# A scan-and-experts kernel: the first block laid out anew

The first of six blocks of a fused kernel gets another order of loads, gates, scans and weight sums, and some buffers of its own.

## The chip, the cores and the metric

One core of one Trainium2 chip. The metric is the device time of one execution in microseconds (us), the median of several runs. The profiled execution has a span some 1.7 us below its run's time.

## The reference, cut to what matters

```python
# batch 4, 8 heads, 768 positions, head_dim 32, state 16
for each chunk: y = (C B^T * decay_mask) x + C state * decay; state = decay_full * state + B^T x * decay
x = y rearranged to (3072, 256)
p = probs / (probs.sum(-1) + 1e-9)
out = sum over 4 experts e of p[:, e] * (relu(x @ w1[e]) @ w2[e])      # w1: 256x1024, w2: 1024x256
```

All in fp32.

## The kernel before

Tokens are handled in 24 chunks of 128 positions; four chunks are a block. The first block's chunks 0 to 3 are computed first. Then come 48 steps; each does half an expert for one block with seven products in place of eight for each of the two multiplications (sums and differences of the quarters are multiplied). Step n does the seven products of its own first multiplication (`fmul`, into the accumulator banks X and Y) and seven of the second multiplication of step n−1 (`smul`). During steps 0 to 7 the chunks of the next block are computed in between: a chunk "enters" in one step (decays, scores, masking) and "leaves" in a later one (outputs, state). The weights' sums are made by GpSimd in the first block, two steps ahead, and stored for the later blocks.

The names: `LT` is the decay mask of a chunk, made by a scan on VectorE; `bdec` and `cts` are two products of it on GpSimd; `masked` multiplies the scores into it; `sums` makes `yS`, the differences of the block's input quarters; `snap` is a copy by ScalarE (ACT).

```python
    def load_decays(c, queue):
        ab = load.tile([P, NH * P], FP32, tag="ab", name="ab")
        ah = load.tile([HN, P], FP32, tag="ah", name="ah")
        cut, whole = (a, a) if c < DIRECT else (acut_d, ac_d)
        nc.sync.dma_start(out=ab, in_=cut[c].rearrange("h s -> (h s)").partition_broadcast(P))
        queue.dma_start(out=ah, in_=whole[c].unsqueeze(1).to_broadcast([NH, N, P]))
        st[c].update(ab=ab, ah=ah)
    # ...
    def sum_weights(n):

        if n >= SPB:
            return
        for op in (lambda w: wt1[n][:, w].rearrange("p (j m) -> p j m", j=JJ),
                   lambda w: w2_op(n, w)):
            nc.gpsimd.tensor_add(op(S1), op(S3), op(A22))
            nc.gpsimd.tensor_sub(op(S2), op(S1), op(A11))
            nc.gpsimd.tensor_sub(op(S4), op(A12), op(S2))
            nc.gpsimd.tensor_sub(op(S3), op(A11), op(S3))
        nc.gpsimd.dma_start(out=w1_d[n], in_=wt1[n])
        nc.gpsimd.dma_start(out=w2_d[n], in_=wt2[n])
    # ...
    def decays(c):
        s = st[c]
        if c < DIRECT:
            clip(s["ab"])
            nc.vector.memset(s["ab"].rearrange("p (h s) -> p h s", h=NH)[:, :, 0:1], 0.0)

        LT = att.tile([P, NH * P], FP32, tag="LT", name="LT")
        nc.vector.tensor_tensor_scan(
            out=LT, data0=s["ab"], data1=ident.rearrange("p h s -> p (h s)"), initial=0.0,
            op0=ALU.mult, op1=ALU.add)
        s["LT"] = LT.rearrange("p (h s) -> p h s", h=NH)

        if c < DIRECT:
            clip(s["ah"])

        s["dec"] = dec = att.tile([HN, P], FP32, tag="dec", name="dec")
        nc.vector.tensor_tensor_scan(
            out=dec, data0=s["ah"], data1=zeros, initial=1.0, op0=ALU.mult, op1=ALU.add)
        s["bdec"] = bdec = att.tile([P, NH, N], FP32, tag="bdec", name="bdec")
        nc.gpsimd.tensor_mul(
            bdec, s["xb"][:, OB:OB + HN].rearrange("p (h n) -> p h n", h=NH),
            s["LT"][:, :, P - 1:P].to_broadcast([P, NH, N]))
        s["cts"] = cts = att.tile([HN, NT, P], FP32, tag="cts", name="cts")
        nc.gpsimd.tensor_mul(cts, s["ctm"], dec.unsqueeze(1).to_broadcast([HN, NT, P]))
    # ...
    def masked(c, qs):
        s = st[c]
        for q in qs:
            h = slice(NT * q, NT * q + NT)
            nc.vector.tensor_mul(s["LT"][:, h], s["g"][q], s["LT"][:, h])
    # ...
    def fmul(n, i):

        k = n // SPB
        f = first.setdefault(n, {})
        bank = "X" if i in (1, 6, 7, 4) else "Y"
        if i in (1, 2, 5):
            f[bank] = ps_f.tile([P, JJ, HB], FP32, tag=bank, name=bank)
        y, Y = yT[k], yS[k]
        w = (A11, A12, S4, A22, S1, S2, S3)[i - 1]
        b1, b2 = slice(0, HB), slice(HB, BLK)
        rhs = (y[:, 0, b1], y[:, 1, b1], y[:, 1, b2], Y[:, 3], Y[:, 0], Y[:, 1], Y[:, 2])[i - 1]
        for j in range(JJ):
            nc.tensor.matmul(
                out=f[bank][:, j], lhsT=wt1[n][:, w, j * P:j * P + P], rhs=rhs,
                start=(i in (1, 2, 5) and j == 0), stop=(j == JJ - 1), skip_group_check=True)
    # ...
    def total(n, i, b):

        z = first[n]["z" + b] = ffn.tile([P, JJ, HB], FP32, tag="z", name="z", bufs=3)
        nc.vector.tensor_add(z, first[n]["Y"], first[n][i])

    def gated(n, b, src):

        if n not in hid:
            hid[n] = {}
        h = hid[n][b] = ffn.tile([P, JJ, HB], FP32, tag="h" + b, name="h" + b)
        k, e = n // SPB, n % SPB // JJ
        half = int(b[1]) - 1
        g = gate[k, e].rearrange("p c s -> p (c s)")[:, half * HB:half * HB + HB]
        nc.vector.scalar_tensor_tensor(
            out=h, in0=first[n][src], scalar=0.0, in1=g.unsqueeze(1).to_broadcast([P, JJ, HB]),
            op0=ALU.max, op1=ALU.mult)

    def diff(n, o, x, y):
        h = hid[n]
        h[o] = ffn.tile([P, JJ, HB], FP32, tag="h" + o, name="h" + o)
        nc.vector.tensor_sub(h[o], h[x], h[y])
    # ...
    for c in range(CPB):
        masks(c)
        scores(c, [(ps_s, f"acc{q}") for q in range(NQ)])
        decays(c)
        added(c, ps_f, "X")
        masked(c, range(NQ))
        outputs(c, ps_f, "Y")
        carry(c)
        if c == 0:
            load_decays(1, nc.sync)
            sum_weights(0)
        if c == 1:
            gates()
            sum_weights(1)
        if c == 2:
            load_gate(0, 0)
        load_chunk(c + 2)
    sums(0)

    both = nc.sync, nc.sync
    for n in range(NS + 1):
        k, r = divmod(n, SPB)
        i, odd = divmod(r, 2)
        c = CPB * (k + 1) + i
        more = c < NCH
        ending = r == 0 and k > 0
        run = n < NS
        if run:
            e = r // JJ
            if r % JJ == 0 and n + JJ < NS:
                load_gate(*divmod(n // JJ + 1, E))
            if n + 2 < NS:
                load_weights(n + 2)
                sum_weights(n + 2)
            fmul(n, 1)
            snap(n, 1)
            fmul(n, 2)
            total(n, 1, "11")
            gated(n, "11", "z11")
        if more and not odd:
            masks(c)
            decays(c)
        if r == 1 and k > 0:
            leave(k - 1, 0, BLK, both)
        smul(n - 1, 1)
        if run:
            fmul(n, 6)
            snap(n, 6)
        smul(n - 1, 3)
        if ending:
            keep(k - 1, 0)
        if more and odd:
            outputs(c, ps_att, "att")
            added(c, ps_att, "att")
        if run:
            fmul(n, 5)
            fmul(n, 7)
            snap(n, 7)
            total(n, 7, "22")
        smul(n - 1, 7)
        smul(n - 1, 5)
        if ending:
            keep(k - 1, 1)
        if run:
            gated(n, "22", "z22")
        if more and odd:
            carry(c)
            if c + 2 < NCH:
                load_chunk(c + 2)
        if run:
            fmul(n, 3)
            total(n, 6, "12")
            fmul(n, 4)
            gated(n, "21", "X")
            gated(n, "12", "z12")
            if more and r == SPB - 1:
                sums(k + 1)
        smul(n - 1, 6)
        # ... (the end of a block's output: cut)
        if run:
            diff(n, "T3", "22", "12")
        smul(n - 1, 2)
        if more and not odd:
            scores(c, ((ps_att, "att"), (ps_att, "att"), (ps_f, "X"), (ps_f, "Y")))
            masked(c, (2, 3, 0, 1))
        smul(n - 1, 4)
        if run:
            diff(n, "T1", "12", "11")
            diff(n, "T2", "22", "T1")
            diff(n, "T4", "21", "T2")
        # ... (output: cut)
```

## Time and profile before

| | before |
|---|---|
| median of runs | 689.91 us |
| profiled span | 687.0 us |
| start of step 0, 1, 2, 3 | 38.02, 54.79, 70.01, 83.39 us |
| first sum of yT (`yS`) | 38.56 us |
| PE busy, VectorE busy | 644.4, 500.4 us |

The median is over four runs; the prediction had three of them, with a median of 690.4. A step's start is the start of its first product, X<-yT. The slices, stretches and waits are shown in the prediction. One more view belongs here, because the prediction did not read it: the groups of VectorE instructions in steps 1 to 3 (54.79 to 96.69 us), shapes kept apart. Columns: line, engine, operation, output<-inputs, shapes, count, busy us, mean ns of one, idle before them and releasers.

```profile
L370 DVE SCALAR_TENSOR_TENSOR h<-z,gate 128x512 f32<-128x512 f32 x9 | 8.3, 919 | 0.2
L360 DVE TENSOR_TENSOR z<-Y,snap 128x512 f32<-128x512 f32 x9 | 6.2, 686 | 8.8 <-ACT snap L355 8.4 <-PE Y L348 0.4
L377 DVE TENSOR_TENSOR hT<-h,hT 128x512 f32<-128x512 f32 x6 | 5.0, 828 | 0.2
L377 DVE TENSOR_TENSOR hT<-h,h 128x512 f32<-128x512 f32 x7 | 4.7, 699 | 0.1
```

All four move the same number of elements. The z row reads one operand from the accumulators and takes 686 ns. The rows that read two tiles of SBUF take up to 919. In this kernel that costs little, because VectorE has 8.8 us of idle time before z in the same steps.

### The profile page before, as it was taken

The numbers are of one execution on the slowest core, as the hardware profiler recorded it, in microseconds if no ns is written. First come the engines' busy times: TensorE is split into PE (matmuls) and PEld (weight loads), VectorE is DVE, ScalarE is ACT, GpSimd is POOL, SyncE is SP. The second block draws the span as 40 slices with busy tenths as digits, with TensorE's granted clock in tenths as the row PEclk, the third lists the DMA queues.
The fourth block names the chain that finished last, engine by engine and source line by source line (L and its number), as shares of the span: only waits on it lengthen the run. The fifth ranks groups of instructions, "written<-read, shape, count | busy, mean of one in ns | idle before, by whom it ended". The sixth has DMA issues, their size and how long they took to land.

```text
span 687.0 us, 9082 instructions
## 1 busy us (share of the span) xinstructions
PE 644.4 (94%) x3465; PEld 539.0 (78%) x3465; DVE 500.4 (73%) x823; ACT 116.1 (17%) x230; POOL 112.4 (16%) x161
## 2 busy tenths in 40 slices
PE   2478999999999999999999999999999999999995
PEld 1246887887888887888887888888888888888884
DVE  4875976878877768768668868769777785856654
ACT  1111111112111112211212211212111122111110
POOL 5636658202000002000002000000100000200000
PEclk9998999999999999999999999999999999999998
DMA  8778487763665464655554574753673453563301
GB/s 286 270 244 318 146 299 253 265 234 115 207 230 196 139 209 171 214 183 187 203 176 161 156 280 137 250 180 124 178 267 138 153 195 111 152 230 108 107 1 31
DMA packets 71482, 128.90 MB, mean 188 GB/s; under 512 B 29072, under 2 KB 53008, under 8 KB 71440
## 3 DMA queue, kind: packets, MB, share of 16 engines
q1 hardware_dynamic: 66232, 112.93, 49.0%
q0 software_dynamic: 2304, 14.68, 5.4%
q10 hardware_dynamic: 2904, 0.72, 0.4%
q8 instruction: 27, 0.44, 0.3%
q14 instruction: 15, 0.12, 0.1%
HBM read 110.25 MB, written 18.07 MB: 187 GB/s over the span
## 4 chain that ended last, share of the span: by engine, by line
PE 88%; DVE 3%; DMA 2%; POOL 1%; issue 0%; SPq 0%; DVEq 0%; POOLq 0%
PE acc L392 41%; PE X L348 24%; PE Y L348 18%; DMA wt<-in_w_dram 2%; PE g L256 2%; PE y L295 2%; DVE h L370 1%; PE y L288 1%; DVE LT L224 1%; DVE LT L266 0%; DVE u L412 0%; POOL wt L145 0%; POOL wt L144 0%; PE A L277 0%; POOL wt L146 0%
## 5 line engine op out<-in xcount | busy, mean ns | idle before, releaser
L360 DVE TENSOR_TENSOR z<-Y,snap 128x512 f32<-128x512 f32 x144 | 99.1, 688 | 132.2 <-ACT snap L355 110.2
L392 PE MATMUL acc<-hT,wt 128*128 128x256 f32 x768 | 191.1, 382 | 0.0
L355 ACT COPY snap<-X 128x512 f32<-128x512 f32 x144 | 84.3, 585 | 487.9 <-PE X L348 485.9
L392 PEld LDWEIGHTS acc<-hT,wt 128*128 128x128 f32 x768 | 144.3, 190 | 25.2 <-issue 6.3
L392 PE MATMUL acc<-h,wt 128*128 128x256 f32 x576 | 148.3, 380 | 4.9 <-DVE u L412 4.9
L348 PE MATMUL X<-yS,wt 128*128 128x256 f32 x576 | 147.8, 379 | 0.0
L392 PEld LDWEIGHTS acc<-h,wt 128*128 128x128 f32 x576 | 109.1, 190 | 21.9 <-DVE u L412 7.3
L348 PEld LDWEIGHTS X<-yS,wt 128*128 128x128 f32 x576 | 109.5, 190 | 14.9
L370 DVE SCALAR_TENSOR_TENSOR h<-z,gate 128x512 f32<-128x512 f32 x144 | 102.6, 712 | 3.3
L348 PE MATMUL Y<-yT,wt 128*128 128x256 f32 x384 | 100.2, 384 | 2.0 <-DVE z L360 2.0
L348 PEld LDWEIGHTS Y<-yT,wt 128*128 128x128 f32 x384 | 72.7, 193 | 14.4 <-DVE z L360 2.8
L236 POOL TENSOR_TENSOR bdec<-xb,LT 128x128 f32<-128x128 f32 x24 | 10.4, 434 | 399.8 <-issue 185.7
L377 DVE TENSOR_TENSOR hT<-h,hT 128x512 f32<-128x512 f32 x96 | 68.9, 718 | 3.3
L377 DVE TENSOR_TENSOR hT<-h,h 128x512 f32<-128x512 f32 x96 | 65.0, 701 | 1.3
L224 DVE TENSOR_TENSOR_SCAN LT<-ab,ident 128x1024 f32<-128x1024 f32 x24 | 55.7, 2323 | 3.8 <-DMA ab<-acut_d 3.7
L348 PE MATMUL X<-yT,wt 128*128 128x256 f32 x192 | 51.5, 392 | 6.7 <-DVE LT L266 6.7
L348 PE MATMUL Y<-yS,wt 128*128 128x256 f32 x192 | 51.5, 390 | 0.0
L266 DVE TENSOR_TENSOR LT<-g,LT 128x256 f32<-128x256 f32 x96 | 34.0, 416 | 20.9 <-PE g L256 12.3
L348 PEld LDWEIGHTS X<-yT,wt 128*128 128x128 f32 x192 | 37.2, 196 | 12.9 <-DVE LT L266 7.5
L348 PEld LDWEIGHTS Y<-yS,wt 128*128 128x128 f32 x192 | 34.7, 189 | 6.5 <-issue 0.8
L370 DVE SCALAR_TENSOR_TENSOR h<-X,gate 128x512 f32<-128x512 f32 x48 | 33.0, 688 | 5.6 <-PE X L348 5.5
L256 PE MATMUL g<-ctm,xb 32*128 32x256 f32 x192 | 19.9, 473 | 11.6 <-ACT ctm L247 11.5
(65 smaller groups left out, 272.8 us busy)
## 6 DMA issues: line engine op xcount, KB each, us to landing
wt<-w_d SPq DMA_DIRECT2D x80, 896.0 KB, 4.6
w_d<-wt POOLq DMA_DIRECT2D x16, 896.0 KB, 7.8
...
```

Source lines behind the costliest of these rows:

```text
L224: nc.vector.tensor_tensor_scan(out=LT, data0=s["ab"], data1=ident.rearrange("p h s -> p (h s)"), initial=0.0, op0=ALU.mult, op1=ALU.add)
L236: nc.gpsimd.tensor_mul(bdec, s["xb"][:, OB:OB + HN].rearrange("p (h n) -> p h n", h=NH), s["LT"][:, :, P - 1:P].to_broadcast([P, NH, N]))
L256: nc.tensor.matmul(out=g.rearrange("p t s -> p (t s)"), lhsT=s["xb"][k, OBT:OBT + P], rhs=s["ctm"][k].rearrange("p t s -> p (t s)"), start ...
L266: nc.vector.tensor_mul(s["LT"][:, h], s["g"][q], s["LT"][:, h])
L288: nc.tensor.matmul(out=y.rearrange("p t s -> p (t s)"), lhsT=state["M"].rearrange("p q d -> p (q d)"), rhs=s["cts"].rearrange("p t s -> p ...
L295: nc.tensor.matmul(out=y[32 * q:32 * q + 32, t], lhsT=xb[:, h * D:h * D + D], rhs=MT[:, NT * q + t], start=(first and t == 0), stop=True, ...
L348: nc.tensor.matmul(out=f[bank][:, j], lhsT=wt1[n][:, w, j * P:j * P + P], rhs=rhs, start=(i in (1, 2, 5) and j == 0), stop=(j == JJ - 1), ...
L355: nc.scalar.copy(out=s, in_=first[n]["X"])
L360: nc.vector.tensor_add(z, first[n]["Y"], first[n][i])
L370: nc.vector.scalar_tensor_tensor(out=h, in0=first[n][src], scalar=0.0, in1=g.unsqueeze(1).to_broadcast([P, JJ, HB]), op0=ALU.max, op1=ALU. ...
L377: nc.vector.tensor_sub(h[o], h[x], h[y])
L392: nc.tensor.matmul(out=acc[k, u][:, half], lhsT=w2_op(n, w)[:, j], rhs=rhs[:, j], start=(n % SPB == 0 and half == 0 and j == 0), stop=(n % ...
```

## The change

Its intent is to start the expert steps earlier. The gates are computed at once; chunk 1's decays are read directly; loads are split and issued in another order. The masking writes a tile of its own (`MT`) and so no longer waits for bdec; LT gets one buffer. The entering chunk's decays stand ahead of GpSimd's sums. The first two products of step 0 stand between chunk 2's operations. Chunk 4 enters in step 1, not 0.

```diff
@@ -87,7 +87,7 @@
 
 
     st = {}
-    DIRECT = 1
+    DIRECT = 2
 
     def load_tokens(c):
         xb = load.tile([P, W], FP32, tag="xb", name="xb")
@@ -96,11 +96,12 @@
 
     def load_decays(c, queue):
         ab = load.tile([P, NH * P], FP32, tag="ab", name="ab")
-        ah = load.tile([HN, P], FP32, tag="ah", name="ah")
         cut, whole = (a, a) if c < DIRECT else (acut_d, ac_d)
         nc.sync.dma_start(out=ab, in_=cut[c].rearrange("h s -> (h s)").partition_broadcast(P))
-        queue.dma_start(out=ah, in_=whole[c].unsqueeze(1).to_broadcast([NH, N, P]))
-        st[c].update(ab=ab, ah=ah)
+        st[c]["ab"] = ab
+        if c % chunks_per_seq:
+            ah = st[c]["ah"] = load.tile([HN, P], FP32, tag="ah", name="ah")
+            queue.dma_start(out=ah, in_=whole[c].unsqueeze(1).to_broadcast([NH, N, P]))
 
     def load_chunk(c):
         load_tokens(c)
# ... cut ...
@@ -135,35 +141,40 @@
                 "p (a j d m) -> p a j d m", a=2, j=JJ, d=2)[:, a_, :, d]
         return wt2[n][:, w * HB:w * HB + HB].rearrange("p (j m) -> p j m", j=JJ)
 
-    def sum_weights(n):
-
-        if n >= SPB:
-            return
-        for op in (lambda w: wt1[n][:, w].rearrange("p (j m) -> p j m", j=JJ),
-                   lambda w: w2_op(n, w)):
-            nc.gpsimd.tensor_add(op(S1), op(S3), op(A22))
-            nc.gpsimd.tensor_sub(op(S2), op(S1), op(A11))
-            nc.gpsimd.tensor_sub(op(S4), op(A12), op(S2))
-            nc.gpsimd.tensor_sub(op(S3), op(A11), op(S3))
-        nc.gpsimd.dma_start(out=w1_d[n], in_=wt1[n])
-        nc.gpsimd.dma_start(out=w2_d[n], in_=wt2[n])
-
+    def sums_of(op):
+        nc.gpsimd.tensor_add(op(S1), op(S3), op(A22))
+        nc.gpsimd.tensor_sub(op(S2), op(S1), op(A11))
+        nc.gpsimd.tensor_sub(op(S4), op(A12), op(S2))
+        nc.gpsimd.tensor_sub(op(S3), op(A11), op(S3))
+
+    def sum_w1(n):
+
+        if n < SPB:
+            sums_of(lambda w: wt1[n][:, w].rearrange("p (j m) -> p j m", j=JJ))
+            nc.gpsimd.dma_start(out=w1_d[n], in_=wt1[n])
+
+    def sum_w2(n):
+        if n < SPB:
+            sums_of(lambda w: w2_op(n, w))
+            nc.gpsimd.dma_start(out=w2_d[n], in_=wt2[n])
+
+    pr = const.tile([P, T // P, E], FP32, name="pr")
     a_sb = const.tile([NCH * NH // 2, 2, P], FP32, name="a_sb")
-    pr = const.tile([P, T // P, E], FP32, name="pr")
+    nc.scalar.dma_start(out=pr, in_=probs)
     nc.scalar.dma_start(
         out=a_sb, in_=a.rearrange("c h s -> (c h) s").rearrange("(p r) s -> p r s", r=2))
     load_tokens(0)
     load_decays(0, nc.scalar)
-    nc.scalar.dma_start(out=pr, in_=probs)
+    load_tokens(1)
+    load_decays(1, nc.scalar)
 
 
     ident = const.tile([P, NH, P], FP32, name="ident")
     make_identity(nc, ident[:, 0])
     for h in range(1, NH):
         nc.gpsimd.tensor_copy(ident[:, h], ident[:, 0])
-    load_tokens(1)
-    load_weights(0)
-    load_weights(1)
+    load_tokens(2)
+    load_w1(0)
     zeros = const.tile([P, P], FP32, name="zeros")
     nc.vector.memset(zeros, 0.0)
@@ -182,22 +193,24 @@
     def clip(v):
         nc.vector.tensor_scalar(out=v, in0=v, scalar1=1e-6, scalar2=1.0, op0=ALU.max, op1=ALU.min)
 
+
+    total = const.tile([P, T // P, 1], FP32, name="total")
+    nc.vector.reduce_sum(total, pr, axis=mybir.AxisListType.X)
+    nc.vector.tensor_scalar_add(total, total, 1e-9)
+    nc.vector.reciprocal(total, total)
+    nc.vector.tensor_mul(pr, pr, total.to_broadcast([P, T // P, E]))
     clip(a_sb)
 
     a_cut = const.tile([NCH * NH // 2, 2, P], FP32, name="a_cut")
     nc.vector.tensor_copy(a_cut, a_sb)
     nc.vector.memset(a_cut[:, :, 0:1], 0.0)
-    nc.scalar.dma_start(
-        out=acut_d.rearrange("c h s -> (c h) s").rearrange("(p r) s -> p r s", r=2), in_=a_cut)
-    nc.scalar.dma_start(
-        out=ac_d.rearrange("c h s -> (c h) s").rearrange("(p r) s -> p r s", r=2), in_=a_sb)
-
-    def gates():
-        total = const.tile([P, T // P, 1], FP32, name="total")
-        nc.vector.reduce_sum(total, pr, axis=mybir.AxisListType.X)
-        nc.vector.tensor_scalar_add(total, total, 1e-9)
-        nc.vector.reciprocal(total, total)
-        nc.vector.tensor_mul(pr, pr, total.to_broadcast([P, T // P, E]))
+    def store_decays():
+        nc.scalar.dma_start(
+            out=acut_d.rearrange("c h s -> (c h) s").rearrange("(p r) s -> p r s", r=2), in_=a_cut)
+        nc.scalar.dma_start(
+            out=ac_d.rearrange("c h s -> (c h) s").rearrange("(p r) s -> p r s", r=2), in_=a_sb)
+
+    def store_gates():
         rows = T // P * E
         pp = ps_att.tile([rows, P], FP32, tag="att", name="pp")
         nc.tensor.transpose(pp, pr.rearrange("p i e -> p (i e)"), ident[:, 0])
@@ -220,24 +233,26 @@
             clip(s["ab"])
             nc.vector.memset(s["ab"].rearrange("p (h s) -> p h s", h=NH)[:, :, 0:1], 0.0)
 
-        LT = att.tile([P, NH * P], FP32, tag="LT", name="LT")
+        LT = att.tile([P, NH * P], FP32, tag="LT", name="LT", bufs=1)
         nc.vector.tensor_tensor_scan(
             out=LT, data0=s["ab"], data1=ident.rearrange("p h s -> p (h s)"), initial=0.0,
             op0=ALU.mult, op1=ALU.add)
         s["LT"] = LT.rearrange("p (h s) -> p h s", h=NH)
-
-        if c < DIRECT:
-            clip(s["ah"])
-
-        s["dec"] = dec = att.tile([HN, P], FP32, tag="dec", name="dec")
-        nc.vector.tensor_tensor_scan(
-            out=dec, data0=s["ah"], data1=zeros, initial=1.0, op0=ALU.mult, op1=ALU.add)
-        s["bdec"] = bdec = att.tile([P, NH, N], FP32, tag="bdec", name="bdec")
-        nc.gpsimd.tensor_mul(
-            bdec, s["xb"][:, OB:OB + HN].rearrange("p (h n) -> p h n", h=NH),
-            s["LT"][:, :, P - 1:P].to_broadcast([P, NH, N]))
-        s["cts"] = cts = att.tile([HN, NT, P], FP32, tag="cts", name="cts")
-        nc.gpsimd.tensor_mul(cts, s["ctm"], dec.unsqueeze(1).to_broadcast([HN, NT, P]))
+        s["MT"] = att.tile([P, NH, P], FP32, tag="MT", name="MT")
+        if c % chunks_per_seq < chunks_per_seq - 1:
+            s["bdec"] = bdec = att.tile([P, NH, N], FP32, tag="bdec", name="bdec")
+            nc.gpsimd.tensor_mul(
+                bdec, s["xb"][:, OB:OB + HN].rearrange("p (h n) -> p h n", h=NH),
+                s["LT"][:, :, P - 1:P].to_broadcast([P, NH, N]))
+        if c % chunks_per_seq:
+            if c < DIRECT:
+                clip(s["ah"])
+
+            s["dec"] = dec = att.tile([HN, P], FP32, tag="dec", name="dec")
+            nc.vector.tensor_tensor_scan(
+                out=dec, data0=s["ah"], data1=zeros, initial=1.0, op0=ALU.mult, op1=ALU.add)
+            s["cts"] = cts = att.tile([HN, NT, P], FP32, tag="cts", name="cts")
+            nc.gpsimd.tensor_mul(cts, s["ctm"], dec.unsqueeze(1).to_broadcast([HN, NT, P]))
 
     def masks(c):
@@ -263,7 +278,7 @@
         s = st[c]
         for q in qs:
             h = slice(NT * q, NT * q + NT)
-            nc.vector.tensor_mul(s["LT"][:, h], s["g"][q], s["LT"][:, h])
+            nc.vector.tensor_mul(s["MT"][:, h], s["g"][q], s["LT"][:, h])
 
     state = {}
# ... cut ...
@@ -432,32 +449,59 @@
             for d in range(2):
                 queues[d].dma_start(out=dst[q, d], in_=ot[32 * q:32 * q + 32, d])
 
-
+    def opened(n):
+
+        fmul(n, 1)
+        snap(n, 1)
+        fmul(n, 2)
+
+
+    warm = const.tile([P, 1], FP32, name="warm")
+    nc.scalar.mul(warm, tmask[:, 0:1], tmask[:, 0:1])
+    acc_banks = [(ps_s, f"acc{q}") for q in range(NQ)]
     for c in range(CPB):
         masks(c)
-        scores(c, [(ps_s, f"acc{q}") for q in range(NQ)])
+        if c == 0:
+            store_decays()
+        scores(c, acc_banks)
+        if c == 0:
+            store_gates()
+            load_decays(2, nc.sync)
+            load_w2(0)
+            load_gate(0, 0)
+            load_chunk(3)
+            load_w1(1)
+            load_w2(1)
+        if c == 2:
+            opened(0)
         decays(c)
-        added(c, ps_f, "X")
+        if c:
+            carry(c - 1)
         masked(c, range(NQ))
-        outputs(c, ps_f, "Y")
-        carry(c)
-        if c == 0:
-            load_decays(1, nc.sync)
-            sum_weights(0)
+        added(c, ps_att, "att")
+        outputs(c, ps_att, "att")
         if c == 1:
-            gates()
-            sum_weights(1)
+            load_chunk(4)
+            sum_w1(0)
         if c == 2:
-            load_gate(0, 0)
-        load_chunk(c + 2)
+            load_chunk(5)
+            sum_w2(0)
+    total(0, 1, "11")
+    gated(0, "11", "z11")
     sums(0)
+    carry(CPB - 1)
+    sum_w1(1)
+    sum_w2(1)
+
 
     both = nc.sync, nc.sync
     for n in range(NS + 1):
         k, r = divmod(n, SPB)
-        i, odd = divmod(r, 2)
-        c = CPB * (k + 1) + i
-        more = c < NCH
+
+        enter, exit = ({1: 0, 2: 1, 4: 2, 6: 3}, {2: 0, 3: 1, 5: 2, 7: 3}) if k == 0 else (
+            {0: 0, 2: 1, 4: 2, 6: 3}, {1: 0, 3: 1, 5: 2, 7: 3})
+        c_in, c_out = (CPB * (k + 1) + d[r] if r in d and k < NBLK - 1 else None
+                       for d in (enter, exit))
         ending = r == 0 and k > 0
         run = n < NS
         if run:
@@ -465,30 +509,35 @@
             if r % JJ == 0 and n + JJ < NS:
                 load_gate(*divmod(n // JJ + 1, E))
             if n + 2 < NS:
-                load_weights(n + 2)
-                sum_weights(n + 2)
-            fmul(n, 1)
-            snap(n, 1)
-            fmul(n, 2)
-            total(n, 1, "11")
-            gated(n, "11", "z11")
-        if more and not odd:
-            masks(c)
-            decays(c)
+                load_w1(n + 2)
+                load_w2(n + 2)
+            if n:
+                opened(n)
+                total(n, 1, "11")
+                gated(n, "11", "z11")
+        if c_in is not None:
+            masks(c_in)
+            decays(c_in)
+        if n + 2 < NS:
+            sum_w1(n + 2)
+            sum_w2(n + 2)
         if r == 1 and k > 0:
             leave(k - 1, 0, BLK, both)
         smul(n - 1, 1)
         if run:
+            if n == 0:
+                fmul(n, 5)
             fmul(n, 6)
             snap(n, 6)
         smul(n - 1, 3)
         if ending:
             keep(k - 1, 0)
-        if more and odd:
-            outputs(c, ps_att, "att")
-            added(c, ps_att, "att")
+        if c_out is not None:
+            outputs(c_out, ps_att, "att")
+            added(c_out, ps_att, "att")
         if run:
-            fmul(n, 5)
+            if n:
+                fmul(n, 5)
             fmul(n, 7)
             snap(n, 7)
             total(n, 7, "22")
# ... cut ...
@@ -519,9 +568,9 @@
         if run:
             diff(n, "T3", "22", "12")
         smul(n - 1, 2)
-        if more and not odd:
-            scores(c, ((ps_att, "att"), (ps_att, "att"), (ps_f, "X"), (ps_f, "Y")))
-            masked(c, (2, 3, 0, 1))
+        if c_in is not None:
+            scores(c_in, ((ps_att, "att"), (ps_att, "att"), (ps_f, "X"), (ps_f, "Y")))
+            masked(c_in, (2, 3, 0, 1))
         smul(n - 1, 4)
         if run:
             diff(n, "T1", "12", "11")
```

## The prediction

The marks in the text below stand for rules of the hardware, and a word on the cause of a wait, that no trace or run here shows; what the trace showed beside them is left. The 330 GB/s of the rivals is an estimate from the trace before, which has 336 GB/s from 10 to 20 us.

> **What bounds the kernel now.** I read the page first: busy shares, then the slices.

> ```profile
> PE 644.4 (94%) x3465; PEld 539.0 (78%) x3465; DVE 500.4 (73%) x823; ACT 116.1 (17%) x230; POOL 112.4 (16%) x161
> ...
> PE   2478999999999999999999999999999999999995
> ...
> POOL 5636658202000002000002000000100000200000
> PEclk9998999999999999999999999999999999999998
> ```

> The span is 687.0 us, so the matrix engine (PE) idles 43 us, and the slices (17.2 us each) put most of it in the first four and the end. No change to the first block can win more than the idle and slow-clock time there. Next, the table of stretches, cut by me at the starts of the first expert steps (a step is one half-expert: 14 products of 4 matmuls, 0.86 us each, 12.07 us). Columns: stretch, length, busy time (instructions) of PE, PEld, DVE, ACT, POOL, then clock, DMA share, GB/s.

> ```profile
> 0.00:38.02 38.02, 15.84 (x136) 7.44 (x136) 25.27 (x61) 5.22 (x13) 22.46 (x41) 1.00 0.83 291
> 38.02:54.79 16.77, 9.74 (x40) 6.76 (x37) 10.26 (x16) 2.72 (x6) 8.79 (x12) 0.90 0.67 218
> 54.79:70.01 15.22, 15.22 (x82) 12.84 (x83) 10.55 (x19) 2.13 (x4) 8.45 (x11) 0.88 0.84 308
> 70.01:83.39 13.38, 13.19 (x65) 10.79 (x64) 12.50 (x16) 2.35 (x5) 11.03 (x12) 1.00 0.33 95
> 83.39:96.69 13.30, 13.30 (x76) 11.29 (x75) 8.73 (x15) 2.13 (x4) 7.12 (x10) 1.00 0.81 290
> 96.69:111.39 14.70, 13.09 (x66) 10.66 (x64) 11.23 (x15) 2.35 (x5) 10.41 (x12) 1.00 0.70 247
> ```

> Step 0 starts at 38.02 and takes 16.77 for its first seven products (6 us of work). From 70 us the PE is nearly full. So only what happens before about 70 us can pay, plus one 2 us hole before 111.39. Why the holes exist, from the waits and from the timeline:

> ```profile
> SPq L212 <- DMA p_d<-p_sb: 9.7, 1, 9.7
> ...
> POOL wt L144 <- DMA wt<-in_w_dram: 30.7, 6, 9.9
> ```

> ```profile
> 54.31 1.42 DVE L266 TENSOR_TENSOR LT<-g,LT 128x256 f32<-128x256 f32 x4 [3.60 <-POOL bdec L236]
> 54.79 1.35 PEld L348 LDWEIGHTS X<-yT,wt 128*128 128x128 f32 x4 [5.45 <-DVE LT L266]
> 54.79 2.07 PE L348 MATMUL X<-yT,wt 128*128 128x256 f32 x4 [5.05 <-DVE LT L266]
> ```

> The queue of loads stood 9.7 us behind the gates' store, because the gates were computed after chunk 1. So weights 2 came late; GpSimd's sums of weights 2 waited 9.9 us for them; bdec of chunk 4 stood behind those sums in program order; the masking, which overwrites LT, waited for bdec; and step 1's products waited for the masking, as the scores sat in their banks X and Y. The chain of waits walks the same way back (DMA of weights, eight POOL sums, POOL bdec, DVE masking, PE at 54.79). Then the PE runs cold: 2.07 us for four matmuls in place of 1.03.

> [...] from 38.02 a matmul takes 634 ns, from 41.42 it takes 379; after the 5.05 us hole it is 631 again. [...] a POOL sum that takes 0.73 alone took 2.76 us from 24.11 beside a scan of 2.28 us from 24.07. [...] Here the DMA share is 0.83 in the first 38 us at 291 GB/s[...]; the hole behind the gates (24 to 31 us) is the exception.

> **The change part by part.** It is all reordering; few operations go (4 scans "dec" of 0.4 us, some GpSimd products of 0.4 to 0.7 us) or come (one clip of ab, 0.69, and its memset, 0.07).

> (a) *Up to the sums of yT.* In the kernel before, the first of them starts at 38.56. VectorE's new order, with durations of the old trace: probs land at about 4.1 (a_sb, first in that queue, landed at 4.16); gates 1.46 → 5.6; a_sb's clip, copy, memset 0.75 → 6.3; clip and memset of ab 0.76 → 7.1; scan 2.29 → 9.4; masking 1.39 → 10.8; chunk 1's clip 0.76, scan 2.3, ah clip and dec 0.9, carry 1.13, masking 1.42 → 17.3; chunks 2 and 3 each scan 2.3, dec 0.4, carry 1.1, masking 1.42 = 5.3 → 27.9; z and h of the early product 1.4 → 29.3. The old kernel's wait of 3.74 for chunk 1's decays goes: they are now read directly, and 2.0 MB have to be moved first, which its own rate of the first slices has done at about 8 to 9 us, before 10.8. On the other engines: ACT makes ctm of a chunk only after the copy of the chunk before; the early product (8 cold matmuls, 3.6 us from 38.02 in the old trace) stands on PE before chunk 2's outputs; and GpSimd's bdec and cts of chunk 3 stand behind the sums of w2(0), 3 to 5 us [...]. Laying these out puts yT of chunk 3 at 30 to 32. I take 30.8: **7.8 us less**.

> (b) *From the sums to step 1.* Before: 54.79 − 38.56 = 16.2. Now four products of step 0 are not there, nor scan and masking of chunk 4. fmul 5 at +0.45, fmul 6, its copy, fmul 7, its copy, then z22 at +4.9; from z22 to the last read of X the old trace took 3.45 (45.54 to 48.98). Sum 8.4, so step 1 starts at about 39.2: **7.8 less**. No masking stands in its way, and the PE is warm.

> (c) *Step 1.* Before 15.22 = 12.07 + chunk 4's outputs 1.4 + cold 1.7. Now 12.07 + scores 0.64; but VectorE carries three leftover differences (2.1), z and h (1.4), scan and dec (2.8 to 3.7), so z22 comes 0.7 to 1.6 late. About 14.2: **1.0 less**.

> (d) *Step 2* has chunk 4 leaving and chunk 5 entering, 12.07 + 1.3 + 0.64 = 14.0 against 13.38: **0.6 more**. From step 3 on the order is the old one.

> (e) bdec ahead of the sums, and MT apart from LT: the hole before 111.39 (14.70 − 12.07 − 0.64) goes: **2.0 less**.

> Sum: 7.8 + 7.8 + 1.0 − 0.6 + 2.0 = 18.0. **690.4 − 18.0 = 672.4 us**, 2.6% less.

> **The rivals.** *DMA becomes the bound.* By 54.79 the old kernel had moved 14.8 MB. The new one needs weights 1 in place by 39 and weights 2 by 53. Ahead of weights 2 in the queue stand six chunks (5.4 MB), two weight pairs (2.1), gates and small loads (0.9), about two stores of 0.9: with weights 2 some 11 MB, at 330 GB/s done at about 35 us. GpSimd then needs 8 us, so by 44. That hides, with some 9 us to spare; were it not so, the time would be 676 to 682. *The chunk loop stays as slow as it was*, because PE, ACT and GpSimd orders interlock through one buffer each (the score banks, two PSUM buffers for A and y, LT now single): then sums start at 34 to 36, and the time is 675 to 678. For it: VectorE was busy only 25 of the first 38 us. Against it: its old waits there have named causes that the change removes (3.7 for ab, 6.6 for bdec in three waits). *VectorE becomes the bound in steps 1 and 2*: it needs 12 to 14 us per step, so at most 2 us lost. *Better than said*: if the PE warms within the early product and stays so, sums start at 29.5, and the time is 669 to 670.

> **Range and chances.** (a) is uncertain by 2.5 us either way, (b) and (c) by 1.5 each, (e) by 1, which together makes some ±4.5; a little more upward for interlocks. Range 667.5 to 678.0. 2% is 676.6, 4.2 us above the centre. Faster by over 2%: 0.82; within 2%: 0.17; slower: 0.01.

> **What would show it.** (a) the first yS subtraction at 29.5 to 32.5; gates done by 6; no wait of the load queue of 9.7 us for p_d. (b) step 1's first X product at 37.5 to 41, with 379 ns a matmul, released by the gated read of X and not by LT. (c) step 2 at 51 to 55. (d) step 2 lasting 13.5 to 14.5. (e) no PE hole of over 0.5 us between steps 4 and 5. The prediction is wrong if sums start after 34, if GpSimd's sums of weights 1 or 2 wait for a DMA while the PE stands, or if a later step has grown by over 1 us.

## The result

| | before | changed |
|---|---|---|
| median of runs | 689.91 us | 679.85 us |
| profiled span | 687.0 | 677.0 |
| first sum of yT | 38.56 | 32.69 |
| start of step 1, 2, 3, 4 | 54.79, 70.01, 83.39, 96.69 | 44.03, 58.81, 74.81, 88.21 |
| length of step 1, 2, 3, 4 | 15.22, 13.38, 13.30, 14.70 | 14.78, 16.00, 13.40, 13.27 |

The ratio of times is 0.9856, with a 95% interval of 0.9833 to 0.9880. A ratio here is the mean time of one kernel's fast runs over that of the other's of the same rounds, so not quite the ratio of the medians. The kernel is 1.4% faster, 10 us where 18 were forecast, and outside the range of the forecast, which had given a gain of over 2% a chance of 0.82.

The page of the changed kernel, busy shares and slices:

```profile
PE 643.3 (95%) x3465; PEld 538.6 (80%) x3465; DVE 504.7 (75%) x821; ACT 116.2 (17%) x231; POOL 107.9 (16%) x153
...
PE   3779999999999999999999999999999999999995
...
POOL 2976845001000002000002000002000000200000
PEclk9989999999999999999999999999999999999999
```

The first two slices and the fourth are fuller on PE. GpSimd's work is denser in the second to fifth slices (digits 9, 7, 6, 8 against 6, 3, 6, 6) and thinner in the sixth and seventh. The table of stretches, first four pieces of step 0 and its approach, then steps 1 to 4 (columns as in the prediction):

```profile
30.00:33.17 3.17, 1.59 (x26) 0.83 (x26) 2.54 (x6) 0.37 (x1) 3.01 (x5) 0.91 1.01 324
33.17:36.55 3.38, 3.37 (x8) 2.43 (x8) 3.31 (x6) 0.00 (x0) 2.98 (x5) 0.58 0.99 327
36.55:39.75 3.20, 1.13 (x4) 0.68 (x4) 1.29 (x4) 1.17 (x2) 2.80 (x5) 0.95 1.06 406
39.75:43.26 3.51, 3.50 (x8) 2.52 (x8) 1.63 (x2) 0.00 (x0) 3.06 (x5) 0.56 0.75 310
44.03:58.81 14.78, 13.56 (x64) 10.77 (x65) 14.08 (x17) 2.35 (x5) 9.76 (x13) 1.00 0.74 245
58.81:74.81 16.00, 14.70 (x91) 11.84 (x90) 15.57 (x22) 2.72 (x6) 11.24 (x14) 1.00 0.80 278
74.81:88.21 13.40, 13.40 (x75) 11.40 (x76) 10.71 (x15) 2.13 (x4) 9.02 (x13) 1.00 0.98 353
88.21:101.48 13.27, 13.09 (x65) 10.65 (x64) 10.81 (x14) 2.34 (x5) 6.94 (x9) 1.00 0.45 140
```

Two things are to be seen. The clock is at 0.58 and 0.56 in two pieces of step 0. And in step 2 VectorE is busy 15.57 of 16.00 us: it is the engine that sets that step. The groups of VectorE in steps 1 to 3 of the changed kernel (44.03 to 88.21 us) say why:

```profile
L387 DVE SCALAR_TENSOR_TENSOR h<-z,gate 128x512 f32<-128x512 f32 x10 | 10.1, 1009 | 0.2
L394 DVE TENSOR_TENSOR hT<-h,h 128x512 f32<-128x512 f32 x8 | 7.6, 970 | 0.1
L394 DVE TENSOR_TENSOR hT<-h,hT 128x512 f32<-128x512 f32 x6 | 6.6, 1096 | 0.2
L377 DVE TENSOR_TENSOR z<-Y,snap 128x512 f32<-128x512 f32 x9 | 6.1, 683 | 2.8 <-ACT snap L372 2.1 <-PE Y L365 0.5
```

The row that reads an accumulator still takes 683 ns. The three that read two SBUF tiles take 970 to 1096, and the idle time before z has fallen from 8.8 to 2.8 us. Last, the matrix engine's timeline of step 0, of which three rows:

```profile
33.17 2.07 PE L365 MATMUL Y<-yS,wt 128*128 128x256 f32 x4 [0.95 <-DVE yS L343]
...
39.75 2.07 PE L365 MATMUL Y<-yT,wt 128*128 128x256 f32 x4 [1.40 <-DVE z L377]
...
44.03 1.13 PE L365 MATMUL X<-yT,wt 128*128 128x256 f32 x4 [0.78 <-DVE h L387]
```

Two products take 2.07 us, where 1.03 to 1.13 is the full-clock time of four matmuls. Step 1 is released by the gated read of X, as forecast, and not by a masking.

### The profile page after: what moved, and what is told of

Read it like the earlier page. It is cut to its first block, busy times and chain, and to the rows that moved or that the text cites. A ratio compares the mean times of both kernels' runs of the same rounds, so it can differ in the third digit from the quotient of the medians.

```text
span 677.0 us, 9047 instructions
## 1 busy us (share of the span) xinstructions
PE 643.3 (95%) x3465; PEld 538.6 (80%) x3465; DVE 504.7 (75%) x821; ACT 116.2 (17%) x231; POOL 107.9 (16%) x153
## 4 chain that ended last, share of the span: by engine, by line
PE 89%; DVE 6%; issue 0%; ACT 0%; POOL 0%; DMA 0%; DVEq 0%
PE acc L409 41%; PE X L365 24%; PE Y L365 19%; DVE h L387 2%; PE y L310 2%; PE g L271 2%; PE y L303 1%; DVE hT L394 1%; DVE LT L237 1%; DVE z L377 0%; DVE u L429 0%; PE A L292 0%; ACT snap L372 0%; DVE MT L281 0%; DVE ot L445 0%
## 5 line engine op out<-in xcount | busy, mean ns | idle before, releaser
L409 PEld LDWEIGHTS acc<-h,wt 128*128 128x128 f32 x576 | 108.9, 190 | 21.8 <-DVE u L429 7.3
L387 DVE SCALAR_TENSOR_TENSOR h<-z,gate 128x512 f32<-128x512 f32 x144 | 104.5, 726 | 3.3
L394 DVE TENSOR_TENSOR hT<-h,h 128x512 f32<-128x512 f32 x96 | 66.8, 719 | 1.3
L244 POOL TENSOR_TENSOR bdec<-xb,LT 128x128 f32<-128x128 f32 x20 | 8.3, 413 | 343.8 <-issue 181.9
L281 DVE TENSOR_TENSOR MT<-g,LT 128x256 f32<-128x256 f32 x96 | 33.9, 414 | 10.5 <-PE g L271 10.4
```

Source lines behind the costliest of these rows:

```text
L244: nc.gpsimd.tensor_mul(bdec, s["xb"][:, OB:OB + HN].rearrange("p (h n) -> p h n", h=NH), s["LT"][:, :, P - 1:P].to_broadcast([P, NH, N]))
L281: nc.vector.tensor_mul(s["MT"][:, h], s["g"][q], s["LT"][:, h])
L387: nc.vector.scalar_tensor_tensor(out=h, in0=first[n][src], scalar=0.0, in1=g.unsqueeze(1).to_broadcast([P, JJ, HB]), op0=ALU.max, op1=ALU. ...
L409: nc.tensor.matmul(out=acc[k, u][:, half], lhsT=w2_op(n, w)[:, j], rhs=rhs[:, j], start=(n % SPB == 0 and half == 0 and j == 0), stop=(n % ...
```

## The experiments

Theories and rivals. **T1**: step 2 is overloaded, because chunk 4 leaves and chunk 5 enters in it. **T2**: GpSimd's sums stretch VectorE's instructions that read two SBUF tiles. **T3**: the half clock costs step 0 some 3 us. **T4**: bdec behind GpSimd's sums was the greatest loss of the kernel before. **T5**: GpSimd's order delays chunk 3. The rivals are in each expectation. The table of all runs, from their medians and profiles (step starts as above; the kernel before, run again in each set, had medians of 688.7 to 689.7, and the ratios are to those):

| run | median us | ratio to before | first sum | step 1 starts | length of steps 1, 2, 4 |
|---|---|---|---|---|---|
| before | 689.9 | 1 | 38.6 | 54.8 | 15.2, 13.4, 14.7 |
| changed | 679.9 | 0.9856 | 32.7 | 44.0 | 14.8, 16.0, 13.3 |
| a_enter0 | 680.5 | 0.9860 | 33.6 | 49.1 | 15.2, 12.9, 13.3 |
| a_memset (wrong results) | 670.9 | 0.9731 | 31.6 | 40.0 | 13.1, 14.2, 12.9 |
| a_warm | 679.5 | 0.9857 | 33.2 | 45.5 | 14.1, 16.0, 13.3 |
| a_warm2 | 678.0 | 0.9830 | 33.3 | 42.6 | 15.6, 16.0, 13.3 |
| b_bdec_first | 683.0 | 0.9906 | 38.6 | 50.7 | 13.5, 12.9, 12.9 |
| b_mt | 681.8 | 0.9898 | 38.5 | 51.0 | 15.1, 12.9, 13.9 |
| b_gates_first | 693.1 | 1.0063 | 41.2 | 55.6 | 15.2, 14.7, 15.4 |
| b_memset (wrong results) | 678.0 | 0.9833 | 35.0 | 47.5 | 13.5, 12.9, 12.9 |
| a_late | 678.5 | 0.9837 | 34.0 | 46.2 | 13.6, 13.4, 13.4 |
| a_pool_order | 676.4 | 0.9825 | 31.2 | 40.1 | 16.7, 15.1, 13.3 |
| a_halves | 679.9 | 0.9862 | 35.7 | 47.3 | 14.5, 14.4, 12.9 |
| a_no_early | 679.1 | 0.9854 | 33.9 | 45.2 | 14.0, 16.0, 13.3 |
| a_sums_first | 680.1 | 0.9863 | 32.9 | 45.9 | 15.0, 15.6, 12.9 |
| a_asb_first | 681.2 | 0.9879 | 35.3 | 48.6 | 13.1, 16.0, 13.3 |
| a_best | 674.4 | 0.9786 | 31.2 | 41.3 | 14.3, 13.4, 13.3 |
| a_best2 | 677.7 | 0.9827 | 31.5 | 41.9 | 17.2, 13.5, 13.4 |
| a_best3 | 674.0 | 0.9779 | 32.4 | 44.7 | 14.2, 13.5, 13.3 |

Names with a_ start from the changed kernel, those with b_ from the kernel before. The medians are of four to six runs, but the instants and lengths are of the one run that was profiled: in a_pool_order, b_bdec_first and the changed kernel that was the fastest run, in a_best3 and a_enter0 the slowest. All but the two memset runs gave correct results.

### GpSimd's sums taken away: a_memset and b_memset

```diff
-        nc.gpsimd.tensor_add(op(S1), op(S3), op(A22))
-        nc.gpsimd.tensor_sub(op(S2), op(S1), op(A11))
-        nc.gpsimd.tensor_sub(op(S4), op(A12), op(S2))
-        nc.gpsimd.tensor_sub(op(S3), op(A11), op(S3))
+        for o in (S1, S2, S4, S3):
+            for v in (0.0, 0.01):
+                nc.gpsimd.memset(op(o), v)
```

> Changed kernel with GpSimd's sums of weights replaced by two memsets of the same destinations each: wrong results on purpose, same transfers, same waits, GpSimd busy but reading no SBUF. Theory 2 (GpSimd's sums [...] stretch every VectorE instruction with two SBUF inputs in steps 0 to 6): the gated products and differences fall from 0.93 to 0.95 us to 0.69 to 0.72 us, step 1 to about 13.6 to 14.0, step 2 to 14.0 to 14.5, the first sum of yT comes 1 to 2 us earlier than 32.7; whole 3.5 to 6 us less than the changed kernel, 674 to 676 us. Rival (VectorE is slow for another reason, or VectorE is not what sets these steps): durations or step lengths stay, whole within 1 us of 679.9.

> The kernel before with memsets in place of GpSimd's sums (wrong results on purpose), to set beside the changed kernel treated the same, which took 670.9 us. If the sums cost the changed kernel more than they cost the kernel before (the stretched VectorE work lay hidden behind the old holes), this runs at 684 to 688 us, 2 to 6 us under before, so that without the sums the change would be worth 13 to 17 us. Rival (the sums cost both the same 9 us, and the change is worth 10 us either way): 680 to 682 us.

A memset reads no SBUF tile, so this keeps the program's order and transfers and takes the reads away. It is not quite clean: the two memsets, 0.31 us each, are also a little shorter than a sum of 0.73, and the memsets of three of the four destinations do not wait for the load of the weights, as the sums do. The changed kernel so treated took 670.9 us, lower still than expected. Its groups of VectorE in steps 1 to 3 (40.02 to 80.61 us):

```profile
L386 DVE SCALAR_TENSOR_TENSOR h<-z,gate 128x512 f32<-128x512 f32 x10 | 7.1, 706 | 0.2
...
L393 DVE TENSOR_TENSOR hT<-h,h 128x512 f32<-128x512 f32 x8 | 5.3, 688 | 0.1
...
L393 DVE TENSOR_TENSOR hT<-h,hT 128x512 f32<-128x512 f32 x6 | 4.2, 692 | 0.2
```

From 1009, 970 and 1096 ns to 706, 688 and 692: T2 stands. With the counts of these rows the stretch is 10 × 0.303 + 8 × 0.282 + 6 × 0.404 = 7.7 us of VectorE time in three steps, which became 3.6 us shorter. Step 2 falls from 16.0 to 14.2, which the prediction had at 14.0. The stretches of steps 1 and 2 of a_memset (columns as in the prediction) show VectorE busy 12.0 us in each, where the changed kernel needed 14.08 and 15.57:

```profile
40.02:53.08 13.06, 13.06 (x64) 10.89 (x65) 11.96 (x18) 2.35 (x5) 8.76 (x26) 1.00 0.91 331
53.08:67.32 14.24, 14.24 (x91) 11.74 (x90) 12.01 (x22) 2.72 (x6) 7.95 (x24) 1.00 0.82 292
```

Not all of the gain is the stretch: of the 8.0 us between the two profiles, 2.9 lie between the first sum and step 1, where the products of a_memset ran at full clock.

The kernel before, treated alike, took 678.0 us, which contradicts what I expected (684 to 688). Taking the sums away gains even more there (11.9 us against 8.9). But b_memset also shortens the wait of bdec behind the sums: six of its sixteen memsets of weights 2 ran before the load had landed, the rest took 3.17 us after it where the sums took 7.1, and chunk 4's bdec came at 46.15 us in place of 53.85. How much of the 11.9 us is the stretch and how much this is not shown. So the sums do not explain why the two kernels lie only 10 us apart; without them they lie 7 us apart. What it explains is why the forecast *level* of 672.4 was not reached: the forecast charged the new order with durations of an undisturbed VectorE.

### One part alone on the kernel before: b_bdec_first, b_mt, b_gates_first

```diff
  # b_bdec_first
-                sum_weights(n + 2)          # ahead of the step's products
...
             decays(c)
+        if n + 2 < NS:
+            sum_weights(n + 2)
  # b_mt
-            nc.vector.tensor_mul(s["LT"][:, h], s["g"][q], s["LT"][:, h])
+            nc.vector.tensor_mul(s["MT"][:, h], s["g"][q], s["LT"][:, h])    # LT: one buffer
  # b_gates_first: probs loaded first in their queue, and
         scores(c, ...)
+        if c == 0:
+            gates()                         # was: after chunk 1
```

> One part of the change alone, on the kernel before: in each step the decays of the chunk that enters stand ahead of GpSimd's sums of the weights two steps on; nothing else moves. Theory 4 (bdec behind the sums was the greatest single loss of the kernel before): the hole of 5 us before 54.8 goes to under 1 us, the cold clock of step 1 with it, the hole before 111.4 too; 6 to 9 us less than before, 681 to 684 us. Rival (the late weights themselves hold the first step back, so the wait only moves): 1 to 3 us less, 687 to 689 us.

> One part of the change alone, on the kernel before: the masking writes a tile of its own, MT, and no longer overwrites LT (which has one buffer now), so it does not wait for bdec. If that is the second cure of the wait before step 1: hole before step 1 under 1.5 us, 4 to 7 us less than before, 682.5 to 685.5 us. Rival (with bdec still behind the sums, the next scan of LT waits for it, or cts and A come late and the products stand all the same): 687 to 690 us.

> Another part of the change alone, on the kernel before: the gates are computed and stored with chunk 0, not after chunk 1; nothing else moves. If the late gates were what made weights 2 late, the wait of 9.7 us of the load queue falls under 3 us, GpSimd's wait of 9.9 us for weights 2 goes, and the hole before step 1 shrinks from 5 us to under 2: 4 to 8 us less than before, 682 to 686 us. That is much the same gain as that of bdec ahead of the sums alone (6.6 us), so the two parts are two cures of one wait and don't add. Rival (the transfers, not their order, make weights 2 late): 0 to 2 us less.

Either of the first two alone gives 6.6 to 7 of the 10 us. In the timeline of b_mt step 1 waits 1.63 us for the masking, where the kernel before waited 5.05:

```profile
51.02 2.08 PE L349 MATMUL X<-yT,wt 128*128 128x256 f32 x4 [1.63 <-DVE MT L267]
```

They are two cures of one wait: the masking stood behind bdec, and bdec stood behind the sums. T4 holds for the kernel before. The third part refuted what the prediction said of the gates. The wait of the load queue for p_d was indeed gone, but the queue then stood behind the outputs of chunks 1 and 2, which free the buffers of xb for chunks 4 and 5:

```profile
SPq L94 <- PE y L295: 14.7, 2, 8.1
SPq L120 <- PE X L348: 12.0, 1, 12.0
```

Weights 2 were issued at 38.1 us in this run, against 35.4 in the kernel before. Weights 2 stand behind chunk 5 in the queue, and chunk 5's xb can't be loaded before chunk 2's outputs, with or without the gates' wait. (The second row is the wait of the load of weights 3, 6.6 us in the kernel before.) Seen from the first sum, nothing moved: weights 2 were issued 3.1 us ahead of it in both kernels. The 9.7 us that I had read as the cause had merely shortened that other wait. And the part cost time: a_sb, now second in its queue, landed after 6.25 us, where it had landed at 4.16, and everything behind it came later. That its place in the queue is the reason is not shown: in the changed kernel, where it is also second (issued at 1.19 us, landed 5.3 us later, against 3.4 when first in the kernel before), SyncE issued a load of 512 KB at 1.20.

### The parts undone in the changed kernel: a_sums_first, a_no_early, a_enter0

```diff
  # a_sums_first: sum_w1(n + 2), sum_w2(n + 2) directly after the loads, ahead of decays(c_in)
  # a_no_early: opened(0), total(0, 1, "11"), gated(0, "11", "z11") back into step 0
  # a_enter0
-        enter, exit = ({1: 0, 2: 1, 4: 2, 6: 3}, {2: 0, 3: 1, 5: 2, 7: 3}) if k == 0 else (...)
+        enter, exit = {0: 0, 2: 1, 4: 2, 6: 3}, {1: 0, 3: 1, 5: 2, 7: 3}
```

> Changed kernel with GpSimd's sums of the weights two steps on put back ahead of the entering chunk's decays (one part undone). If bdec behind the sums was where the gain came from, the whole rises by 4 to 7 us, 684 to 687 us, with holes ahead of steps that follow an entering chunk (2, 3, 5). Rival (with MT apart from LT the masking no longer waits for bdec, so the order is worth nothing any more): within 1.5 us of 679.9.

> One part of the change undone: the first two expert products of step 0 stand after the first block again, all else as changed. If the early products pay (they fill the matrix engine's idle time in chunk 2 at no cost), the whole is 1 to 3 us more than the changed kernel, 681 to 683 us. Rival (3.7 us of cold products ahead of chunk 2's outputs and 1.8 us of VectorE time ahead of the sums cost what they save): 678.5 to 681 us, first sum of yT at 29.5 to 31.5 and step 1 at 43 to 45.

> One part of the change undone: chunk 4 enters in step 0 again and leaves in step 1, all else as changed. Theory 1 (VectorE is overloaded where chunk 4 leaves and chunk 5 enters in the same step, step 2 of 16.0 us in the changed kernel): step 2 falls to 13.2 to 14.2 us, step 1 stays near 14 to 15; step 0 grows by the scan, dec and masking of chunk 4, 3 to 5 us, so the whole is about level with the changed kernel, 678 to 682 us. Rival (step 2 is long because of something else, a late transfer or the POOL order): step 2 stays at 15.5 to 16 us and the whole is 682 to 685 us.

None of the three moved the time by more than its runs scatter: 680.1, 679.1 and 680.5 against 679.9. With MT apart, bdec's place is worth nothing (the rival of a_sums_first). The early products gain nothing. The two themselves are as cold late as early (2.08 and 1.82 us in a_no_early, 2.07 and 1.91 in the changed kernel), but in a_no_early the five products after them ran at full clock: in its profile PE came to full clock only at 36.85 us and did not lose it again in step 0. The rival there was right on the whole and wrong on the way: the first sum came at 33.9 us, not at 29.5 to 31.5. a_enter0 shows T1 and its price in one profile: step 2 falls from 16.0 to 12.9 us, and step 0 ends 5 us later, in exchange (in that profile all five of its later products ran at half clock, in the changed kernel's two wholly and two in part).

### The clock in step 0: a_warm, a_warm2

```diff
+    def busy(m):                      # useless products into a free accumulator bank
+        d = ps_s.tile([P, 2, HB], FP32, tag="acc3", name="dummy")
+        for j in range(m):
+            nc.tensor.matmul(out=d[:, j % 2], lhsT=ident[:, 0], rhs=..., start=True, stop=True)
     # busy(5) before step 0, busy(3) after snap(0, 6), busy(6) after snap(0, 7); a_warm2: 1, 1, 3
```

> Changed kernel with 14 useless matmuls in three holes of step 0 (5 before the first sum of yT is ready, 3 while X is copied, 6 before product 3), into a bank that is free then. Theory 3 (the matrix engine runs step 0 at half clock because its work there is sparse, which costs about 3 us between the first sum and step 1): products of step 0 take 0.38 us a matmul in place of 0.6, step 1 starts at 41 to 42 in place of 44.0, and the whole is 2 to 3 us less, 677 to 678 us. Rival (VectorE and the copies set step 0, whatever the clock): step 1 still starts at 43.5 to 44.5 and the whole is 679.5 to 680.5.

> As a_warm, with 1, 1 and 3 useless matmul calls in place of 5, 3 and 6: those ran twice as long as meant and stood in the way by 2.6 us before the first sum alone. Theory 3: products of step 0 at 0.38 us a matmul from 36 us on, first sum to step 1 in 9 to 10 us in place of 11.3, step 1 at 42 to 43.3, whole 678 to 679. Rival (clock does not matter in step 0): step 1 at 43.8 to 44.5 and 679.5 to 680.5 us.

a_warm miscarried: each fp32 call became two instructions in the trace (10 for the first 5 calls, 3.81 us), and the dummies stood in the way. a_warm2 is the valid run: step 1 started at 42.6 in place of 44.0, with four of step 0's five remaining products at full clock, and the whole took 678.0 us (677.3 to 678.2, against 678.8 to 681.2). Taking most of the half clock away was thus worth about 1.8 us of the total; T3's mechanism is right, its 3 us were not reached. The gain at step 1 did not reach step 2 whole: step 1 grew from 14.8 to 15.6 us.

### GpSimd's order: a_pool_order

```diff
         if c == 2:
             load_chunk(5)
-            sum_w2(0)
...
     carry(CPB - 1)
+    sum_w2(0)
     sum_w1(1)
```

> Changed kernel with GpSimd's sums of w2(0) moved from before chunk 3's bdec and cts to after them; same work. Theory 5 (those sums, blocked 2.6 us by a scan, held bdec and cts of chunk 3 back, opened a hole of 1.5 us on the matrix engine and so let its clock fall for step 0): bdec of chunk 3 at 27 to 28 in place of 29.8, first sum of yT at 31.5 to 32.2, step 0's products at 0.38 us a matmul, step 1 at 40.5 to 42.5; whole 677 to 678.5 us. Rival (VectorE's own chain sets the first sum, and the clock falls anyway): first sum at 32.5 to 33, step 1 at 43.5 to 44.5, whole 679.5 to 680.5.

The first sum came at 31.2 and step 1 at 40.1, close to the 30.8 and 39.2 of the forecast. The timeline of PE shows full clock, with waits that are no shorter than in the changed kernel:

```profile
32.15 1.13 PE L365 MATMUL Y<-yS,wt 128*128 128x256 f32 x4 [1.69 <-DVE yS L343]
...
37.35 1.13 PE L365 MATMUL Y<-yT,wt 128*128 128x256 f32 x4 [1.40 <-DVE z L377]
...
40.13 1.13 PE L365 MATMUL X<-yT,wt 128*128 128x256 f32 x4 [0.78 <-DVE h L387]
```

Chunk 3's bdec came at 26.2 us in place of 29.8. T5's first half (GpSimd's order delays chunk 3) holds beyond this one profile: the first sum came at 31.2 to 32.4 us in the four runs with the sums of w2(0) put off (a_pool_order, a_best, a_best2, a_best3), and at 32.7 or later in all other runs that start from the changed kernel, but for a_memset.

The second half, that this order keeps the clock up, does not hold for sure. The profiled run is the fastest of five. Three runs took 675.8 to 676.4 us with a mean granted clock of 0.997, and two took 679.4 and 680.1 with 0.993. And the profile of a_best3, whose order up to here differs only in that a_sb is loaded first, has the same wait before the first product after the sums (1.70 us) and half clock after it. That profile is the slowest of its runs, 676.6 us at 0.993; the other three took 672.8 to 674.0 at 0.997. So the full clock in the profile of a_pool_order was in part luck. Its gain over the changed kernel is not certain either: the intervals of the two ratios overlap (0.9800 to 0.9851 and 0.9833 to 0.9880).

Of 3.9 us won at step 1 only 2.9 are left in the span, because step 1 grew by 1.9 us to 16.7, of which step 2 gave 0.9 back:

```profile
40.13:56.82 16.69, 13.57 (x65) 10.81 (x65) 15.82 (x18) 2.35 (x5) 15.27 (x18) 1.00 0.81 296
56.82:71.89 15.07, 14.40 (x91) 11.55 (x89) 14.77 (x21) 2.72 (x6) 11.39 (x15) 1.00 0.78 287
```

VectorE 15.82 and GpSimd 15.27 of 16.69 us: the sums that were put off now collide with step 1. The same sums and the same VectorE work have to be done in any order.

### Less collision: a_late, a_halves, and three combinations

```diff
  # a_late (block 0)
-  ({1: 0, 2: 1, 4: 2, 6: 3}, {2: 0, 3: 1, 5: 2, 7: 3})
+  ({1: 0, 3: 1, 5: 2, 6: 3}, {2: 0, 4: 1, 6: 2, 7: 3})
  # a_halves
+        for j in range(JJ):           # each sum as two of 128x128
+            nc.gpsimd.tensor_add(op(S1)[:, j], op(S3)[:, j], op(A22)[:, j])   # and so on
  # a_best: both, and a_pool_order;  a_best2: a_late, a_pool_order, a_asb_first
  # a_best3: as a_best2, with halves from weights 2 on
  # a_asb_first: a_sb loaded ahead of the probabilities, the gates' VectorE work after a_sb's
```

> Changed kernel with chunks 4, 5, 6, 7 entering in steps 1, 3, 5, 6 and leaving in 2, 4, 6, 7, so that the step in which one leaves and one enters is step 6, after the last of GpSimd's sums, in place of step 2. Theory 1 and 2 together: step 2 falls from 16.0 to 13.2 to 14.0, step 6 rises from 12.9 to 14.0 or 14.3, the rest stays: 1 to 2 us less than the changed kernel, 677.5 to 679 us. Rival (an overlapped step costs 2 to 3 us wherever it lies): step 6 near 15.5, whole 679.5 to 681.

> Changed kernel with each of GpSimd's sums cut into two of 128x128: the same work in instructions of some 0.42 us in place of 0.73. Theory 2 [...]: the gated products and differences fall from 0.93 or 0.95 to 0.80 to 0.88 us, step 2 from 16.0 to 14.8 to 15.6, whole 677 to 679.5 us. Rival [...]: durations as before, 679.5 to 682 us.

> Changed kernel with the decays a_sb loaded ahead of the probabilities, and the gates' VectorE work after a_sb's: a_sb landed 6.5 us in when second, 4.2 us when first. If that holds chunk 0 and 1 back, the first sum of yT comes 0.7 to 1.5 us earlier and the whole falls by as much, 678.3 to 679.2. Rival (ab of chunk 0 or the transfers behind it set chunk 0 and 1): within 0.5 us of 679.9.

> Three edits together on the changed kernel, meant as a better version: sums of w2(0) after chunk 3's bdec and cts; chunks 4 to 7 entering in steps 1, 3, 5, 6; sums in halves. If they add, 3.5 + 1.4 + 1 us less than 679.9, so 673 to 675 us, step 1 at 40 to 41 and step 2 at 13.4 to 14. If they are cures of the same VectorE time, 675 to 677 us.

> Sums of w2(0) after chunk 3's cts, chunks entering in steps 1, 3, 5, 6, and a_sb first; sums whole. If a_pool_order's 3.5 us, a_late's 1.4 us and a_asb_first's 1 us add: 673.5 to 675 us. If the sums in halves made most of a_best's 674.4: 675.5 to 677.

> As a_best2, with GpSimd's sums in halves from weights 2 on only, so that chunks 0 to 3 and step 0 are not delayed by them. Expected under a_best (674.4) by 0.5 to 2 us: 672.5 to 674 us. Rival [...]: 674 to 676 us.

a_late moves the overlapped step to step 6, after the last sums: step 2 takes 13.4 and step 6 takes 13.9 in place of 12.9. T1 needs T2: the overlap costs 2.6 us beside GpSimd's sums and 1 us without them. a_halves shortened the stretch, in steps 1 to 3 from 1009 and 970 ns to

```profile
L388 DVE SCALAR_TENSOR_TENSOR h<-z,gate 128x512 f32<-128x512 f32 x10 | 8.7, 873 | 0.2
...
L395 DVE TENSOR_TENSOR hT<-h,h 128x512 f32<-128x512 f32 x7 | 5.8, 844 | 0.1
```

and steps 1 and 2 to 14.5 and 14.4; but its first sum came at 35.7, so the whole stayed at 679.9. a_asb_first missed: the probabilities, now second in their queue, landed at 7.75 us and VectorE waited 3.14 us for them in its order, ahead of chunk 0's scan.

The combinations a_best and a_best3 beat both kernels, at 674.4 and 674.0 us: 0.9786 (0.9773 to 0.9800) and 0.9779 (0.9757 to 0.9801) of before. The two are not told apart, so the rival of a_best3, that the halves in steps 0 and 1 mattered, is not decided. a_best2 (677.7) lacks the halves, has a step 1 of 17.2 us, and missed both of its forecasts (673.5 to 675, or 675.5 to 677).

## Why the prediction was wrong

It was a sum of five terms. Each against what was measured, with two runs that take causes away (us):

| term | forecast | changed | a_memset | a_pool_order |
|---|---|---|---|---|
| (a) first sum of yT at | 30.8 | 32.7 | 31.6 | 31.2 |
| (b) from there to step 1 | 8.4 | 11.3 | 8.4 | 9.0 |
| (c) step 1 | 14.2 | 14.8 | 13.1 | 16.7 |
| (d) step 2 | 14.0 | 16.0 | 14.2 | 15.1 |
| (e) step 4, without its hole | 12.7 | 13.3 | 12.9 | 13.3 |

The changed kernel missed by 1.9 + 2.9 + 0.6 + 2.0 + 0.6 = 8.0, which is the 18.0 forecast less the 10.0 of the profiles.

- **(a), mis-sized.** "chunks 2 and 3 each scan 2.3, dec 0.4, carry 1.1, masking 1.42 = 5.3" used undisturbed durations; beside GpSimd a scan took 2.92 and a dec 0.88 in the trace. GpSimd's sums of w2(0) held chunk 3's bdec until 29.8 us; a_pool_order took that away and came within 0.4 us of the term (with the profiles' scatter of 1 to 2 us, no closer reading is possible). That a_sb would land only at 6.5 us was missed as well.
- **(b), mis-sized, the largest.** "and the PE is warm" failed. From 33.17 and from 39.75 the products ran at half clock. The profiles of a_memset and a_pool_order, at full clock, give 8.4 and 9.0, close to the forecast's 8.4. That the four runs of a_memset kept it (0.997 to 0.999) and only three of five of a_pool_order did means that the forecast took as given a clock that differs from run to run (see the end of this section).
- **(c) and (d).** "VectorE becomes the bound in steps 1 and 2: it needs 12 to 14 us per step, so at most 2 us lost" was the right rival at the wrong size. The counts of instructions were right; the durations of the products and differences, 0.7, were those of a lone VectorE. It needed 14.08 and 15.57 us, and 12.0 in each step with GpSimd's reads gone (a_memset). The row of 919 ns stood in the trace of the kernel before, and I had not asked for it by shape. I had read GpSimd's loss from the trace (a sum of 2.76 us beside a scan, where others took 0.73), and charged a loss of VectorE's only for scan and dec (2.8 to 3.7).
- **(e)** was right in kind: the hole before step 5 is gone. Step 4 is still 0.3 us longer than in a_memset.
- **The story of the gates** was wrong: b_gates_first is slower than before by 0.6%. The rest of the chain (sums, bdec, masking, products) was right, and b_bdec_first and b_mt show it.
- **The rival of the chunk loop** was set aside on a misreading: of the "6.6 for bdec in three waits" only 3.0 us, in two waits, lie in the first 38 us. The third, of 3.6 us, is the masking of chunk 4 at 54.31. The first sum, at 32.7, came between the forecast (30.8) and this rival (34 to 36).
- **The range** was too narrow. The uncertainties that it names make 3.4 us if they are independent and 6.5 if they add, not 4.5, and term (d), which missed by 2.0, had been given none. The sign that the prediction itself set, a later step grown by over 1 us, came true: step 2 grew by 2.6.
- **Right**: the DMA rival is out, as argued. GpSimd waited 1.4 us in all for weights up to 125 us, against 30.7 before:

```profile
POOL wt L145 <- DMA wt<-in_w_dram: 1.4, 2, 1.2
```

Where the expected gain went, then: at step 1 the changed kernel is 10.8 us ahead of before; that is less than the forecast 15.6 by the clock and by chunk 3's delay. It is 6.6 us ahead of b_bdec_first at step 1 (44.0 against 50.7), but 2.3 us ahead at step 3 (74.8 against 77.1). In steps 1 and 2 GpSimd is about as busy in both kernels (18.3 of 26.4 us in b_bdec_first, 21.0 of 30.8 in the changed kernel). VectorE has 35 instructions and 21.8 us of work in b_bdec_first, and 39 with 29.7 us in the changed kernel: more work in the two steps, in longer instructions (0.76 us in the mean against 0.62, shapes mixed). Without idle time, VectorE gives the lead back.

What stays open: why the clock fell in step 0 in some runs and not in others. No run was made to test it. In the profiles of a_memset, a_no_early, a_pool_order, a_best and a_best2 the first product after the sums ran at full clock, in those of the changed kernel, a_late, a_enter0, a_halves, a_sums_first, a_asb_first and a_best3 at half. In the changed kernel it fell with no hole over 1.54 us in the 5 us before 33.17. The order alone does not decide it, since the runs of one kernel differ (0.993 and 0.997 in a_pool_order and in a_best3).

Two such windows each of the changed kernel, a_pool_order and a_best3 (columns: stretch, length, PE busy, clock, DMA share, GB/s):

```profile
29.18:32.59 3.41, 1.59 (x26) 1.00 0.94 308
32.59:36.00 3.41, 2.83 (x7) 0.50 1.00 331
...
28.39:31.80 3.41, 2.07 (x26) 1.00 0.74 240
31.80:35.22 3.42, 2.40 (x10) 1.00 0.72 188
...
30.10:33.51 3.41, 1.71 (x19) 1.00 0.67 229
33.51:36.93 3.42, 3.42 (x8) 0.50 1.01 353
```

The hole before the first product after the sums lies across an edge of the grid in a_pool_order (busy 0.61 and 0.70) and within one window in a_best3 (0.50). These are counts, and not a rule: no run was made to see whether an order that leaves PE busier in each such window keeps the clock. The clock column also reads 1.00 before the record begins (25.76 us in the changed kernel), where products at 21.51 us took 2.07 us: it does not show the first cold stretch.
